# A gated MLP beside a long convolution: the filter's transposition moved from TensorE to DMAs, and the last down-projections split into column pairs

## The chip, the cores and the metric

The kernel runs on one core of one Trainium2 chip. The metric is device time in microseconds. The kernel before has a median of 190.6 us over 3 runs (190.31 to 190.84).

The engines that matter are TensorE (PE in the profile, its weight loads are PEld), VectorE (DVE), ScalarE (ACT), GpSimd (POOL) and SyncE (SP). Each executes its own instructions in the order in which they were written and waits on semaphores. DMAs are issued from SP, ACT or, in the changed kernel, also from POOL; a queue's issues stand in the order of the issuing engine's program.

## The reference

One input x of 2048 rows by 512 is normalised, and two branches use it:

```python
xn = layernorm(x)                                  # x = A_q, [1, 2048, 512]
# branch A: a 4-tap shift of k, times v, then a long causal convolution along the rows
kv = shift4(k, shift_k) * v
y  = irfft(rfft(pad(kv)) * rfft(pad(ssm_k)))[:2048] + kv * ssm_D
s  = xn * y
# branch B: a gated MLP, 512 -> 1792 -> 512
g  = silu((gelu(xn @ w_gate) * (xn @ w_up)) @ w_down)
out = x + s * g
```

The filter `ssm_k` is stored with its 512 channels as rows and the 2048 time steps as columns. The convolution works on tiles with time in partitions, so the filter has to be transposed before its first use.

## The kernel before, in words

**The gated MLP.** The 2048 rows are worked in four quarters q = 0 to 3 of 512. For each quarter and each of 14 column blocks m, `unit` (line 1190) runs four 128x512 matmuls with `Wg` and four with `Wu`, a GELU on ACT and a product on DVE that writes `HT`. The product reads the second matmul's result straight from PSUM (line 1203) or, for the units in the list UNITS, from a copy that ACT makes (line 1200). The first two units of q 0 are cut into 128-column matmuls. `down` (line 1206) then runs 14 matmuls with `Wd` for each of four row tiles. `Wd` comes in two loads, blocks 0 to 6 and 7 to 13. In the last quarter the last tile is done as 384 and 128 columns. In all there are 642 matmuls of 512 columns in gate, up and down, beside 14 of 384, 14 of 128, and the 64 of 128 of the first two units.

**The convolution.** It is done as a transform in two stages. Stage 1 (`stage1`, lines 950 and 959) multiplies data with time in partitions by the table `F1`, as two halves of 64 rows: 32 matmuls for the filter (H, from `HTr`) and 32 for kv (K, from `V`). ACT or DVE moves the results to SBUF; they go to DRAM scratch (`ZH` by ACT's queue, `ZK` by SP's) and come back regrouped as `BH` and `BK`. Stage 2 runs 16 passes of 16 small matmuls with the table `TF` (line 1028). Products of the spectra on DVE (lines 1131, 1154), eight inverse passes of 32 small matmuls, the scratch `ZI`, and 32 matmuls of 128x64 with `G1` (line 1270, called y here) end it. `kshift` (lines 1005 to 1013) makes kv on DVE: 28 operations of 128x2048, four groups of seven, the last of each group reading one load of v.

**The filter's transposition before.** Four loads bring `ssm_k` to `Hn` with channels in partitions. `h_transpose` (line 916) transposes it on TensorE, two bf16 values at a time as one fp32 value, 32 transposes of 128x128 into PSUM; five DVE and three ACT copies of 128x1024 bring it to `HTr`. A DVE operation on one partition (line 930, the fold) adds `ssm_D`.

**What sets the order.** Every piece of work is a task; the string SEQ lists all tasks in the order in which they are written into the engines' programs, and the table LAND holds the times at which a planner takes the loads to land. The string ORDER sets the order of the loads. The tracker `Trk` writes each engine's waits from the tiles that an instruction reads and writes. In the planner, loads are tasks of an engine of their own; in the program they are issued by SP, in one queue with its other DMAs.

The lines that carry matmuls through the helper `mm` all show as L642, and copies through `copy` as L633 (ACT) and L636 (DVE).

Of the kernel before, what the change touches and what calls it, by code (L numbers as in the profile page):

```python
# [25 lines left out]
ORDER = "x00 h0 x01 w0 D0 h1 w1 h2 h3 s0 k0 w2 x1 k1 k2 w3 d0 d1 v0 v1 k3 v2 v3 x2 x3"  # L26
SEQ = (
# [265 lines left out]
class Sched:  # L293
# [55 lines left out]
    def run(self):  # L349
# [4 lines left out]
        for name in SEQ.split():  # L354
# [17 lines left out]
            elif t.nbytes:  # L372
                en = t.end
                if eng == "ACT":
                    for l in order:
                        if l.eng == "loads" and l.end > t.start + 4300.0 and t.start < 48000.0:
                            l.end += self.TAKEN * min(1.0, (l.end - t.start - 4300.0) / 1000.0)
# [37 lines left out]
def build_kernel(nc, A_q, A_k, A_v, A_shift_k, A_ssm_k, A_ssm_D, B_w_gate, B_w_up, B_w_down, out):  # L415
    with ExitStack() as es0:
# [56 lines left out]
        top = place["at"]  # L473
        assert top <= 229344, top

        Hn = at("Hn", [128, KD, S_LEN], BF16, g_at)
        HTr = at("HTr", [128, NT // 2, 2 * DM], BF16, kk_at - 16384)
        skr_at = kac_at + 8192
        SKR = at("SKR", [128, DM * 4], BF16, skr_at)
# [131 lines left out]
        def psl(b):  # L611
            return b.slot
# [744 lines left out]
```

## Time and profile before

| what | value |
|---|---|
| median of 3 runs | 190.6 us |
| span of the profiled execution | 189.2 us |
| PE busy | 182.8 us, 97% |
| DVE busy | 165.5 us, 87% |
| ACT busy | 141.6 us, 75% |
| POOL busy | 10.4 us, 5% |
| moved by DMAs | 47.84 MB, mean 253 GB/s |

The span runs from the first to the last recorded instruction of the execution. The median of the runs is 1.4 us above it. "Busy" counts the time in which an engine has an instruction in work; overlapping instructions of one engine are counted once. The granted TensorE clock is 1.00 throughout but for the last slice. In the chain of work that ended last each piece is followed back to what released it. DMA rows give the microseconds from issue to landing.

### The profile page before, as it was taken

The page shows a single profiled execution, that of the slowest core. Times are in us where ns is not written, and L with a number is a line of the kernel's source. Part 1 is how long each engine was busy: PE and PEld are TensorE (multiplying, and loading weights), DVE is VectorE, ACT ScalarE, POOL GpSimd, SP SyncE. Part 2 cuts the span into 40 slices and gives each one's busy share as a digit, 9 for nine tenths or more (in the row PEclk, how much of TensorE's full clock was granted, in tenths as well). Part 3 has the DMA queues.
Part 4 walks back from the last instruction along what each step waited for, and adds up shares of the span by engine and source line. Part 5 has one row for each costly group of instructions (what it writes and reads, how often), then busy time and mean ns, then how long its engine had stood idle before and what let it go on. Part 6 is the DMA issues. An engine that isn't in the chain of part 4 may idle for free.

```text
span 189.2 us, 3591 instructions
## 1 busy us (share of the span) xinstructions
PE 182.8 (97%) x1406; PEld 80.6 (43%) x1418; DVE 165.5 (87%) x250; ACT 141.6 (75%) x196; POOL 10.4 (5%) x26
## 2 busy tenths in 40 slices
PE   7899999999999999999999999999999999999992
PEld 2685544544333334334444443433333344444441
DVE  6889999999999999978589599999999964658695
ACT  3749797998879798799638897998999575323971
POOL 5312302000000000022000000000000000000000
PEclk9999999999999999999999999999999999999998
DMA  5999999999584996557999997499345254908754
GB/s 177 319 381 297 366 380 360 402 415 297 166 309 150 335 287 229 166 187 235 301 310 173 333 322 251 144 299 326 135 162 170 97 181 146 376 36 283 268 186 153
DMA packets 36422, 47.84 MB, mean 253 GB/s; under 512 B 7347, under 2 KB 26039, under 8 KB 36406
## 3 DMA queue, kind: packets, MB, share of 16 engines
q1 hardware_dynamic: 29878, 39.23, 63.6%
q10 hardware_dynamic: 6528, 8.39, 12.8%
q8 instruction: 11, 0.18, 0.4%
q14 instruction: 5, 0.04, 0.1%
HBM read 27.39 MB, written 14.68 MB: 222 GB/s over the span
## 4 chain that ended last, share of the span: by engine, by line
PE 79%; DVE 15%; ACT 3%; issue 2%
PE psall L642 67%; PE psall L1028 6%; DVE KTM L1009 3%; DVE KAC L1011 2%; PE psall L916 2%; PE psall L950 2%; DVE HT L1203 1%; DVE G L1299 1%; PE psall L959 1%; PE psall L1270 1%; DVE G L1287 1%; DVE XN L965 1%; DVE G L1238 1%; DVE G L1237 1%; ACT XN L870 1%
## 5 line engine op out<-in xcount | busy, mean ns | idle before, releaser
L642 PE MATMUL psall<-xnT,Wu 128*128 128x512 bf16 (+1 forms) x248 | 56.0, 359 | 0.0
L642 PE MATMUL psall<-xnT,Wg 128*128 128x512 bf16 (+1 forms) x248 | 55.3, 359 | 0.5 <-DVE xnT L636 0.5
L642 PE MATMUL psall<-Wd,HT 128*128 128x512 bf16 (+2 forms) x226 | 50.3, 366 | 1.2 <-issue 0.8
L1194 ACT ACTIVATE GE<-psall 128x512 bf16<-128x512 f32 x54 | 31.7, 605 | 10.5 <-PE psall L642 10.0
L1203 DVE TENSOR_TENSOR HT<-psall,GE 128x512 bf16<-128x512 f32 x43 | 29.1, 685 | 8.0 <-PE psall L642 7.8
L642 PEld LDWEIGHTS psall<-xnT,Wu 128*128 128x128 bf16 x248 | 22.5, 98 | 26.0 <-issue 2.3
L642 PEld LDWEIGHTS psall<-xnT,Wg 128*128 128x128 bf16 x248 | 21.7, 98 | 26.7 <-issue 2.3
L642 PEld LDWEIGHTS psall<-Wd,HT 128*128 128x128 bf16 x238 | 21.4, 98 | 27.4 <-issue 5.4
L633 ACT ACTIVATE BO<-psall 128x1024 bf16<-128x1024 f32 x22 | 22.0, 1024 | 9.6 <-PE psall L1270 5.8
L1131 DVE TENSOR_TENSOR HSW<-KB,HSW 128x2048 bf16<-128x2048 bf16 x16 | 19.2, 1217 | 0.0
L633 ACT ACTIVATE HSW<-psall 128x1024 bf16<-128x1024 f32 x16 | 15.5, 1036 | 2.3 <-PE psall L1028 2.2
L633 ACT ACTIVATE KB<-psall 128x1024 bf16<-128x1024 f32 x14 | 13.8, 1028 | 2.6 <-PE psall L1028 2.4
L1011 DVE TENSOR_TENSOR KAC<-KAC,KTM 128x2048 bf16<-128x2048 bf16 x12 | 14.6, 1216 | 0.1
L1009 DVE TENSOR_TENSOR KTM<-KK,SKB 128x2048 bf16<-128x2048 bf16 x12 | 14.6, 1214 | 0.1
L633 ACT ACTIVATE AST<-psall 128x1024 bf16<-128x1024 f32 x12 | 12.3, 1023 | 1.9 <-PE psall L950 1.5
L1227 ACT ACTIVATE G<-psall 128x512 bf16<-128x512 f32 x12 | 7.2, 597 | 5.7 <-PE psall L642 4.5
L849 DVE BATCH_NORM_STATS2 stats<-X 128x6 f32<-128x512 bf16 x16 | 10.6, 672 | 0.5 <-DMA X<-in_A_q_dram 0.5
L1229 DVE SCALAR_TENSOR_TENSOR G<-G,psall 128x512 bf16<-128x512 bf16 x12 | 8.1, 680 | 3.0 <-ACT G L1227 3.0
L1131 DVE TENSOR_TENSOR KB<-KB,HSW 128x2048 bf16<-128x2048 bf16 x8 | 9.6, 1220 | 0.1
L1154 DVE TENSOR_TENSOR HSW<-HSW 128x2048 bf16<-128x2048 bf16 x8 | 9.5, 1217 | 0.0
L862 POOL TENSOR_TENSOR mv<-mv,NHALF 128x1 f32<-128x1 f32 (+1 forms) x7 | 5.3, 754 | 70.7 <-DVE mv L860 66.1
L633 ACT ACTIVATE X<-psall 128x1024 bf16<-128x1024 f32 x8 | 8.1, 1018 | 1.1 <-PE psall L959 1.0
(88 smaller groups left out, 163.4 us busy)
## 6 DMA issues: line engine op xcount, KB each, us to landing
BH<-ZH SPq DMA_DIRECT2D x8, 512.0 KB, 5.9
BK<-ZK SPq DMA_DIRECT2D x8, 512.0 KB, 5.8
HSW<-HSW SPq DMA_DIRECT2D x16, 256.0 KB, 3.1
ZI<-BO ACTq DMA_DIRECT2D x16, 256.0 KB, 2.9
BI<-ZI SPq DMA_DIRECT2D x8, 512.0 KB, 5.0
ZK<-AST SPq DMA_DIRECT2D x6, 512.0 KB, 3.4
Hn<-in_A_ssm_k_dram SPq DMA_DIRECT2D x4, 512.0 KB, 7.5
KK<-in_A_k_dram SPq DMA_DIRECT2D x4, 512.0 KB, 10.7
```

Of the source, the lines that this page charges most:

```text
L633: return h.activation(o, i, ACTF.Copy, scale=scale)
L642: return h.matmul(o, lhsT=l, rhs=r, start=st, stop=sp)
L849: t_stats[t] = op([("DVE", 670.0)], lambda e, h, t=t: h.bn_stats(stats[:, t, :], X[:, t, :]), r=[bX[q][t % 4]], w=[bst[t]], rr=[R_X[t]], w ...
L1009: op([("DVE", dur)], lambda e, h, j=j, m=m: h.tensor_tensor(KTM[:, m.slot, :, :], kk(j), sk(j), ALU.mult), r=need + [bSKB[j], a], w=[m], r ...
L1011: op([("DVE", dur)], lambda e, h, m=m: h.tensor_tensor(KAC[:, a.slot, :, :], KAC[:, a.slot, :, :], KTM[:, m.slot, :, :], ALU.add), r=[m], ...
L1028: trk.op("PE", lambda h: h.matmul(ps(s, i)[b, :], lhsT=wt(col)[a, :], rhs=data(col)[a, :], start=n < 16, stop=n >= len(todo) - 16, tile_po ...
L1131: return hd.tensor_tensor(pair(KB, *(2 * DM * z for z in slots())) if to else x, k, x, ALU.mult)
L1154: return hd.tensor_tensor(x, x, y, ALU.add)
L1194: op([("ACT", act(512))], lambda e, h: h.activation(GE[:, g.slot, :], bank(pg), ACTF.Gelu_apprx_tanh), r=[pg], w=[g], rr=lambda: R_bank(pg ...
L1203: op([("DVE", dve(512, 1))], lambda e, h: h.tensor_tensor(HT[:, q % 2, m, :], bank(pu), GE[:, g.slot, :], ALU.mult), r=[pu, g], w=[bHT[q][m]],
L1227: op([("ACT", act(n))], lambda e, h, g=g, pc=pc: h.activation(g, pc(), ACTF.Tanh, scale=0.5), r=[p], w=[bt], rr=lambda p=p: R_bank(p), ww= ...
L1229: op([("DVE", dve(512, 1))], lambda e, h, g=g, pc=pc: h.scalar_tensor_tensor(out=g, in0=g, scalar=1.0, in1=pc(), op0=ALU.add, op1=ALU.mult ...
```

## The change

1. **The filter's transposition.** The identity in fp32, the 32 transposes on TensorE and the eight copies to `HTr` go. Eight DMAs on SP's queue read `ssm_k` from DRAM, 128 channels by 1024 time steps (256 KB) each, and transpose it on the way into `HTT`, which lies in tiles 8 to 15 of `X` and `XN`. Two DMAs issued by POOL store `HTT` (1 MB each) to a new DRAM scratch `ZT`, and two more, which wait for both stores, load it back as `HTr` with the time steps regrouped (1 MB each). `HTr` now lies where `G` is later. The filter's stage 1 takes plain 512-column tiles, so its PSUM copies need no reordering.

2. **The last down-projections.** In the last quarter each 128x128 block of weights is split in two 128x64 blocks that go to the two column halves of the array, as y does. This holds for the 42 matmuls of 512 columns and the 14 of 384 columns; the 14 of 128 columns stay.

3. **The order.** ORDER, SEQ and LAND are new, and some dependencies between tasks are looser (the products of q 1 no longer wait for the filter's stage 1).

What the new order does on the engines:

- On TensorE the first K passes (8 matmuls, from v's first load) stand behind 128 and 140 of the 512-column gate and up matmuls, and the filter's stage 1 behind 152 to 200 of them; before, the filter's stage 1 stood behind 4 to 127 gate, up and down matmuls. The first down-projection (blocks 0 to 3) stands behind 196, its blocks 4 to 13 behind 200. The first stage-2 pass stands behind 287 (before 260), the last inverse pass behind 547 (before 534), the first y behind all 600 and eight paired matmuls (before behind 600).
- On DVE the fold stands behind 19 of the 28 kshift operations and 18 products of full units.
- On SP, the order of the loads is x, w0, x, D, w1, taps, halo, k0, h0, w2, h1, k1, h2, x1, h3, w3, h4, k2, h5, k3, h6, v0, h7. Behind h7 stand two stores `ZK<-AST`, which wait for ACT's copies of the first two K stage-1 results, and behind these the loads v1, v2, v3, wd0 and wd1. Before, all loads but the last two x stood ahead of the first `ZK` store.
- On POOL the four new DMAs stand behind the layernorm step of quarter 1 and ahead of those of quarters 2 and 3.

The core of the diff:

```diff
-ORDER = "x00 h0 x01 w0 D0 h1 w1 h2 h3 s0 k0 w2 x1 k1 k2 w3 d0 d1 v0 v1 k3 v2 v3 x2 x3"
+ORDER = "x00 w0 x01 D0 w1 s0 k0 h0 w2 h1 k1 h2 x1 h3 w3 h4 k2 h5 k3 h6 v0 h7 v1 v2 v3 d0 d1 x2 x3"
...
-        Hn = at("Hn", [128, KD, S_LEN], BF16, g_at)
-        HTr = at("HTr", [128, NT // 2, 2 * DM], BF16, kk_at - 16384)
+        HTr = at("HTr", [128, NT, DM], BF16, g_at)
+        HTT = [T[:, 8:16, :] for T in (X, XN)]
...
+        ZT = nc.dram_tensor("ZT", [S_LEN, DM], BF16, kind="Internal")
...
-        def load_h(k, ring):
-            load(f"h{k}", Hn[:, k, :], h_dr[:, k, :], [R_Hn[k]], [bHn[k]], 524288, ring)
+        def load_h(i):
+            h, k = i // KD, i % KD
+
+            def f(e):
+                o = HTT[h][:, :, 128 * k:128 * k + 128]
+                trk.dma("SP", lambda g: g.dma_start(out=o, in_=h_dr[:, k, 1024 * h:1024 * h + 1024], transpose=True), d_htt[i], w=[R_HTT[h][k]])
+            last_load[0] = S.add([("loads", T_ISSUE)], f, w=[bHTT[h][k]], nbytes=262144, land=float(LAND[f"h{i}"]))
...
-        def h_transpose(k):
...
-                        trk.op("PE", lambda h, o=o, src=src: h.transpose(o, src, ident32[:]), r=[R_Hn[k], R_id32], w=R_bank(pp[hf]), accum=True)
...
-                    return copy(e, h, HTr[:, 4 * hf:4 * hf + 4, 256 * k:256 * (k + 1)], bank16(pp[hf]).rearrange("p (t x) -> p t x", x=256))
...
+        for h in range(2):
+            def st(e, h=h):
+                dst = bass.AP(ZT, 1024 * h * DM, [[DM, 128], [128 * DM, 8], [1, DM]])
+                dma("POOL", dst, HTT[h], d_zt[h], R_HTT[h], [R_Z["T"][h]])
+            S.add([("POOL", P_ISSUE)], st, r=bHTT[h], w=[bZT[h]], nbytes=1048576)
+        d_htr = [dsem(f"d_htr{h}") for h in range(2)]
+        for h in range(2):
+            def ld(e, h=h):
+                src = bass.AP(ZT, 8 * h * DM, [[16 * DM, 128], [DM, 8], [1, DM]])
+                dma("POOL", HTr[:, 8 * h:8 * h + 8, :], src, d_htr[h], R_Z["T"], R_HTr[8 * h:8 * h + 8])
+            S.add([("POOL", P_ISSUE)], ld, r=bZT, w=[bHTr[h]], nbytes=1048576)
...
-            af = (down_tasks[q - 2] if q >= 2 else []) + (s1_tasks["H"] if q == 1 else [])
+            af = down_tasks[q - 2] if q >= 2 else []
...
+                        paired = q == NQ - 1 and c1 - c0 > 128
...
+                                if paired:
+                                    for i in range(2):
+                                        c = slice(64 * i, 64 * i + 64)
+                                        trk.op("PE", lambda h, m=m, i=i, c=c: h.matmul(pc()[c, :], lhsT=HT[:, q % 2, m, 128 * jt + 64 * i:128 * jt + 64 * i + 64], rhs=Wd[:, m, c0:c1], start=m == 0, stop=m == MF - 1, tile_position=(0, 64 * i)),
+                                               r=[R_HT[q % 2][m], R_Wd[m // 7]], w=R_bank(p), accum=True)
+                                    continue
```

More of the change, by code (lines that the diff above doesn't have):

```diff
@@ L373, in run @@
                 en = t.end
-                if eng == "ACT":
+                if eng in ("ACT", "POOL"):
                     for l in order:
                         if l.eng == "loads" and l.end > t.start + 4300.0 and t.start < 48000.0:
-                            l.end += self.TAKEN * min(1.0, (l.end - t.start - 4300.0) / 1000.0)
+                            l.end += self.TAKEN * t.nbytes / 500000.0 * min(1.0, (l.end - t.start - 4300.0) / 1000.0)
                 if eng == "SP":
@@ L559, in build_kernel @@
         R_KTM = [res(f"KTM{j}", KTM[:, j, :, :]) for j in range(1)]
-        R_Hn = [res(f"Hn{k}", Hn[:, k, :]) for k in range(KD)]
-        R_HTr = [[res(f"HTr{t}_{k}", HTr[:, t, 256 * k:256 * k + 256]) for k in range(KD)] for t in range(NT // 2)]
+        R_HTT = [[res(f"HTT{h}_{k}", T[:, :, 128 * k:128 * k + 128]) for k in range(KD)] for h, T in enumerate(HTT)]
+        for rh in R_HTT:
+            for r in rh:
+                for o in rh:
+                    if o is not r:
+                        r.ovl.remove(o)
+        R_HTr = [res(f"HTr{t}", HTr[:, t, :]) for t in range(NT)]
         R_SKR = res("SKR", SKR[:])
@@ L655, in build_kernel @@
         bWd = [B(f"Wd{i}") for i in range(2)]
-        bHn = [B(f"Hn{k}") for k in range(KD)]
-        bHTr = [[B(f"HTr{k}_{h}") for h in range(2)] for k in range(KD)]
+        bHTT = [[B(f"HTT{h}_{k}") for k in range(KD)] for h in range(2)]
+        bZT = [B(f"ZT{h}") for h in range(2)]
+        bHTr = [B(f"HTr{h}") for h in range(2)]
         bHD = B("HD")
@@ L926, in build_kernel @@
-        for k in range(KD):
-            h_transpose(k)
-        HT0 = HTr[0:1, 0, :].rearrange("p (d c) -> p c d", c=2)[:, 0, :]
+        d_zt = [dsem(f"d_zt{h}") for h in range(2)]
+        for h in range(2):
[4 more added lines that the diff above has]
+        d_htr = [dsem(f"d_htr{h}") for h in range(2)]
@@ L942, in stage1 @@
             a = B(f"A{x}{u}", pAST[x])
[L943 removed]
+            af = [] if x == "H" else kshift_tasks[:1] + [t_table]
             pp = [B(f"ps1{x}{u}_{i}", pC) for i in range(2)]
[L945 to L952 removed]
@@ L953, in stage1 @@
[L953 to L964 removed]
+            data, rdata = (HTr, R_HTr) if x == "H" else (V, R_V)
@@ new lines, in stage1, with halves @@
+            bdata = [bHTr[u // 4]] + ([bFold] if u == 0 else []) if x == "H" else [bKV[u // 2]]
+            bl = B(f"low{u}")
+            for i in range(2):
+                def halves(e, i=i):
+                    for b in range(2):
+                        k = slice(64 * b, 64 * b + 64)
+                        trk.op("PE", lambda h, b=b, k=k: h.matmul(ps(psl(pp[i]), b), lhsT=F1[k, :], rhs=data[k, 2 * u + i, :], start=True, stop=True, tile_position=(64 * b, 0)),
+                               r=[R_F1, rdata[2 * u + i]], w=[R_ps[psl(pp[i])][b]], accum=True)
+                s1_tasks[x].append(S.add([("PE", T_FWD)], halves, r=[bF1] + bdata, w=[pp[i]], lat=150.0, mode=2))
@@ L965, in stage1 @@
+            for i in range(2):
+                p = pp[i]
+                op(EV(1024), lambda e, h, p=p, i=i: copy(e, h, ast[x][a.slot][:, :, i, :], ps(psl(p)).rearrange("p (b d) -> p b d", b=2)), r=[p], w=[a] + ([bl] if x == "H" else []),
+                   rr=lambda p=p: R_ps[psl(p)], ww=lambda: [R_AST[x][a.slot]], after=af)
+            if x == "H":
                 op([("DVE", dve(1024, 2))], lambda e, h: h.tensor_tensor(ast[x][a.slot][:, 1, :, :], ast[x][a.slot][:, 1, :, :], ast[x][a.slot][:, 0, :, :], ALU.add), r=[bl], w=[a],
@@ L966, in stage1 @@
                    rr=lambda: [R_AST[x][a.slot]], ww=lambda: [R_AST[x][a.slot]])
-            for i in range(2 if x == "K" else 0):
-                p = pp[i]
-                op(EV(1024), lambda e, h, p=p, i=i: copy(e, h, ast[x][a.slot][:, :, i, :], ps(psl(p)).rearrange("p (b d) -> p b d", b=2)), r=[p], w=[a],
-                   rr=lambda p=p: R_ps[psl(p)], ww=lambda: [R_AST[x][a.slot]], after=af)
             def st(e):
```

68 lines of the change are left out of this document (17 added, 51 removed), and 44 rows, old and new, of the table SEQ.

## The prediction

> **What bounds the kernel now.** I read the page first, then the chain that ended last, the groups by line and window, and SP's own queue with its landings.
>
> ```profile
> span 189.2 us, 3591 instructions
> PE 182.8 (97%) x1406; PEld 80.6 (43%) x1418; DVE 165.5 (87%) x250; ACT 141.6 (75%) x196; POOL 10.4 (5%) x26
> ...
> by line: PE psall L642 66.8%; PE psall L1028 5.5%; DVE KTM L1009 3.0%; DVE KAC L1011 2.4%; PE psall L916 2.2%; PE psall L950 2.0%; issue 1.7%; DVE HT L1203 1.3%; DVE G L1299 1.1%; PE psall L959 1.1%; PE psall L1270 1.1%; DVE G L1287 1.0%; D
> ...
> 8.70 1.96 PE psall L642 x32
> 10.66 0.22 PE psall L892 x4
> ...
> 19.15 0.54 PE psall L959 x4
> ...
> 23.36 0.76 PE psall L959 x6
> 24.11 9.20 PE psall L642 x42
> ...
> 36.51 1.13 DVE KTM L1009
> 37.64 0.34 DVE HT L1200
> 37.98 1.14 DVE KAC L1011
> 39.11 0.60 DVE HT L1203
> ...
> 56.05 1.67 PE psall L642 x7
> ```
>
> TensorE is busy nearly throughout, and the chain is on it except from 35.8 to 56.05 us, where it runs through VectorE (kshift between the products of the units), and in the last ten microseconds. A 512-column matmul costs 9.20/42 = 0.219 us, a quarter matmul 1.96/32 = 0.061, a stage-1 group of four 0.54 and of six 0.76.
>
> ```profile
> 0.00:15.00 15.00, 13.27 (x111) 8.76 (x111) 11.98 (x36) 7.96 (x16) 4.89 (x19) 1.00 0.88 299
> 0.00:30.00 30.00, 28.27 (x196) 16.50 (x197) 26.53 (x58) 20.97 (x33) 7.32 (x23) 1.00 0.97 322
> 33.00:45.00 12.00, 11.81 (x70) 5.30 (x70) 12.00 (x18) 11.46 (x19) 0.00 (x0) 1.00 1.04 368
> 88.00:101.00 13.00, 12.68 (x101) 5.39 (x102) 9.88 (x17) 7.94 (x12) 1.01 (x1) 1.00 1.09 291
> 20.00:80.00 60.00, 59.71 (x306) 25.28 (x309) 59.83 (x81) 51.64 (x75) 1.36 (x2) 1.00 0.86 296
> 82.85:154.90 72.05, 71.42 (x781) 28.64 (x788) 63.51 (x83) 58.86 (x76) 2.02 (x2) 1.00 0.74 227
> 154.90:186.00 31.10, 30.58 (x169) 13.78 (x168) 22.29 (x35) 16.37 (x23) 0.00 (x0) 1.00 0.62 217
> ```
>
> After the length come the busy times of PE, weight loads, DVE, ACT and POOL, the granted clock, the DMA share and GB/s. Three resources are full at once early: DMAs to 45 us (9.7 MB by 30 us, then 368 GB/s), DVE from 20 to 80 us (59.8 of 60), PE always. So an edit that frees PE early gains only as far as DVE and the DMAs let the work move up.
>
> **The change, part by part.** The frame is the profiled execution: PE ends at 185.75 (its last row below), the span at 189.2, the median 1.4 above the span. I re-time PE's order by stretches and keep those 3.45 us of tail.
>
> *Transposes off TensorE.*
>
> ```profile
> L916 PE MATMUL psall<-ident,Hn 128*128 128x128 f32 x24 | 3.7, 285 | 0.0
> ...
> L636 DVE COPY HTr<-psall 128x1024 bf16<-128x1024 bf16 x5 | 3.3, 682 | 0.2 <-PE psall L916 0.2
> ...
> L849 DVE BATCH_NORM_STATS2 stats<-X 128x6 f32<-128x512 bf16 x4 | 2.5, 674 | 0.0
> ...
> L986 POOL COPY SKB<-SKR 128x512 bf16<-128x512 bf16 x4 | 2.4, 654 | 7.6 <-DMA SKR<-in_A_shift_k_dram 7.6
> ```
>
> The chain gives this line 2.2% of the span, 4.2 us over 32 transposes; the first two rows here are of 8.7 to 56.05 us, the statistics of 15 to 52. That is the most that PE can gain. But the first eight run while nothing else is ready, before quarter 0 is normalised, so I leave PE's first gate matmul at 8.70. From there to the filter's first pass PE has 64 quarter matmuls (3.9), 152 matmuls (33.3), 24 transposes of xn (0.055 each, 1.3) and two K groups (1.1): 48.3 us. DVE loses the five copies, and reaches the fold after 19 kshift operations (1.14 each, 21.7), 18 products (eleven of 0.60, seven of 0.34, 9.0) and some 4.5 us of layernorm (four statistics are 2.5 of it). It starts when taps and the first k are there: 3.5 MB of loads are 11.7 us at the 299 GB/s of the first 15, 2.0 to land (below), 2.4 for POOL's copies of the taps, 16 us. So the fold is at 51: DVE is level with PE, so this is the earliest, not a cushion.
>
> *The filter's new path.*
>
> ```profile
> 31.20 1.86 SPq L615 DMA_DIRECT2D V<-in_A_v_dram  x2
> 33.11 3.05 SPq L1039 DMA_TRANSPOSE MI<-TFA  x1
> ...
> 48.42 1.21 SPq L1039 DMA_TRANSPOSE MI<-TFB  x1
> 57.61 0.41 SPq L615 DMA_DIRECT2D ZK<-AST  x1
> ...
> 88.57 4.88 SPq L884 DMA_TRANSPOSE xnT<-XN  x1
> ...
> ZH<-XN ACTq DMA_DIRECT2D x4, 512.0 KB, 3.4
> ...
> Wd<-in_B_w_down_dram SPq DMA_DIRECT2D x2, 896.0 KB, 13.7
> ...
> 169.88 1.94 ACT L633 ACTIVATE BO<-psall 128x1024 bf16<-128x1024 f32 x2 [1.71 <-PE psall L1270]
> ```
>
> A transposing DMA takes SP 1.21 us for 128 KB and 4.88 for 512 KB, so 2.44 for each of the eight, 19.5 in all against 0.41 for a plain one. SP can have issued h7 near 30 us; the data come later. Up to h7 the loads are 10.35 MB, plus the first 1.05 MB store. With 9.66 MB by 30 us and 368 GB/s after, that is moved by 34.7. The window from 88 to 101 us, with two transposes of xn among plain DMAs, moved 291 GB/s at full DMA share: 13 x (1 - 291/368) = 2.7 us lost for 1.05 MB, so 5.4 for the filter. I take half (other gaps may be in that window): 37.4, and 2.0 to land (3.4 of a 512 KB store less 1.4 of moving): 39.4. Then the second store and the first load, one after the other: 1.05 MB at 368 GB/s is 2.85, with 2.0 fixed 4.9 each, and 0.4 to issue each: HTr's first half lands at 50 (47 to 53). I take PE's first filter pass at 50, 1.7 after it could.
>
> The Trainium skill (Advanced Engine Details and Errata, X-Bar Transpose) says that transposing DMAs on this chip are as fast as regular ones. By that the 2.7 fall away, HTr lands at 47.3 and PE loses nothing here; the window's 291 GB/s speaks for some loss.
>
> *Loads behind a wait.* This is the edit that decides. On SP two ZK stores now stand before v1 to v3 and wd0, wd1, and they wait for the first K results. By DVE, kv of the first group is ready 8.7 us before the fold (six kshift operations, 6.8; four products, 1.9), at 42.3; two K groups with 12 matmuls between end at 46.2; ACT's last two copies take 1.9: the stores go out at 48.5, the loads by 52, where the loads before were all issued by 33. They carry 4.45 MB (ZK 1.05, v 1.57, Wd 1.83). Beside them run HTr's second half (1.05) and ZH stores: 7.1 MB with three of these, 19.2 us at 368 GB/s; wd1 lands near 69, 63 if it has all of the bandwidth, 72 with five ZH stores. The stores will not give way: ZH lands in 3.4 us beside loads that take 13.7. PE wants wd1 after 48 more matmuls (10.5) and the 32 filter matmuls (4.2), at 50 + 14.7 = 64.7. The bounds are 0 and 7; I take 4.0, near the upper sum. DVE's later uses of v1 to v3 (from 65 us) are covered.
>
> *To the end.* From there to the first stage-2 pass 87 matmuls (19.1) and six K groups (3.2): 22.3. The middle, first stage-2 pass to last inverse, took 72.05 us with 274 matmuls; it now has 260: minus 3.1, 69.0. DVE then fills 63.5 of 69 less some regrouping and ACT 58.9; the cover is thin, so 0 to 2 for the range.
>
> ```profile
> 169.19 1.00 PEld L1270 LDWEIGHTS psall<-BI,G 128*64 128x64 bf16 x12 [0.42 <-DVE HT L1203]
> ...
> 182.09 3.66 PE L642 MATMUL psall<-Wd,HT 128*128 128x512 bf16 x29
> ...
> 169.26 1.42 PE psall L1270 x12
> ...
> 174.67 0.60 PE psall L1270 x4
> ```
>
> *Column pairs.* Twelve y matmuls took 1.42 and four 0.60, so a further pair costs (1.42 - 0.60)/4 = 0.205 us, no more than one full matmul, with two weight loads of 1.00/12 = 0.083 each inside. The 56 pairs cost nothing; for the 384-column ones the loads (0.167) and columns (0.164) are level. The entry to a y group, 0.60 - 0.41 = 0.19, falls away four times: -0.7. The tail is 30.85 (154.9 to 185.75), less 13 matmuls (2.85) and 0.7: 27.3.
>
> The Trainium skill (TensorEngine Tiling (Array Packing), Restrictions) says that column tiling disables Fast Weight Load, which speaks against pairs; the y rows above, which pay for it already, show no loss in pace.
>
> *Sum.* 50 + 14.7 + 4.0 + 22.3 + 69.0 + 27.3 = 187.3 against 185.75: +1.55. On the median: 192.2 us.
>
> **The rivals.**
>
> *The loads arrive in time.* If wd1 takes the bandwidth first (63 us), nothing waits at the first down-projection and the sum is 183.3, or 181.6 with HTr before 48.3: 2.4 to 4.1 faster, 186.5 to 188.2. For it: once h7 has landed the queue of loads is empty, so the filter's store and load have the DMAs to themselves. Against it: the ZH stores start just as the loads do. It decides at 64.7 us for wd1.
>
> *The regrouping is late.* The four DMAs are POOL's first here, in a stretch where DVE is never idle. No row prices their issue; a POOL copy of 0.65 us is one end. If each of the three in the chain (second store, two loads) waits for one or two DVE operations of 1.14, the first half lands 2.3 to 5 us later, at 52 to 55, and the fold holds up DVE, which has nothing to spare. By 55, the Wd wait shrinks to nothing, since PE then asks at 69.7, and the sum is 188.3, to 190 if the second half is late too: 193 to 195.5.
> The Trainium skill (SBUF — State Buffer, SBUF: two separate sides) has this as a rule: POOL's DMA descriptors are held up while DVE runs two-port operations. No run here shows it yet.
>
> *The pairs do not overlap.* Then 42 x 0.219 + 14 x 0.164 = 11.5 us more, 203.7. The y rows speak against it.
>
> **How the numbers follow.** Late Wd loads 0.48, loads in time 0.33, late regrouping 0.14, serial pairs 0.03, the rest for faults in the middle. About 0.3% (0.6 us) is what a measurement can tell from no change. Of the first, 0.05 ends within that and 0.03 below; of the second 0.03 ends within. Faster 0.30 + 0.03 = 0.33, within 0.3% 0.05 + 0.03 = 0.08, slower 0.40 + 0.19 = 0.59. The likeliest gives 192.2, its own range 190 to 195. The range over the first three is 187 to 196.5: below it lie only loads and HTr both at their earliest, above it serial pairs.
>
> **What would show it.** The line of the fp32 transposes is gone and DVE's copies to HTr too. In SP's queue the first ZK store stands near 48 us and wd1's issue after it, with a wait on ACT. PE idles before its first Wd matmuls (64 to 70 us), released by a DMA of Wd; in the first rival that idle time is nil, in the second PE and the fold wait for HTr. The first filter pass is at 50, the first stage-2 pass at 91, the last inverse near 160. The paired rows run at 0.21 to 0.22 us a pair. I am wrong if the first Wd matmul waits for nothing, if transposing DMAs take far more than 2.44 us of SP or throttle the other loads so that Wg and Wu are late from 15 to 30 us, or if the middle does not keep the pace of 72 us for 274 matmuls.

## The result

The changed kernel is slower: 203.5 us median (199.7 to 205.7, 4 runs) against 190.7 us for the kernel before on the same chip, and a ratio of 1.052 with an interval of 1.047 to 1.057. The ratio is taken from the two lower of the four runs, 9.9 us above the kernel before; the two upper ones, of which one is the profiled execution (205.7 us), are left out of it, so the trace below accounts for some 5 us more than the ratio stands for. The forecast was 192.2 us, with a range of 187 to 196.5. The direction was right, though not for the reason given; the size was far too small.

First the page of the profile after. The rows PE and PEclk have one digit for each fortieth of the span, the busy share and the granted clock in tenths.

```profile
span 203.9 us, 3660 instructions
PE 184.5 (90%) x1442; PEld 77.6 (38%) x1442; DVE 165.5 (81%) x250; ACT 136.3 (67%) x188; POOL 13.3 (7%) x29
PE   7799979997089839999999999999999999999993
PEclk9999999999769976999999999999999999999999
```

PE was busy 97% of the span before and is at 90%. It does about as much as before, but it has holes at 50 to 57 us and at 70 to 75 us, and behind each the granted clock is low for some microseconds.

The waits of PE in the profile after (microseconds in total, times, the longest):

```profile
PE psall L950 <- DMA HTr<-ZT: 7.0, 1, 7.0
PE psall L950 <- DVE XN L642: 4.0, 1, 4.0
PE psall L648 <- DMA Wg<-in_B_w_gate_dram: 1.9, 2, 1.5
```

None of them is for `Wd`, the wait on which the forecast was built. The chain of work that ended last (start, length, what) shows how the two long ones come about:

```profile
30.60 9.32 DMA XN<-in_A_ssm_k_dram
...
39.95 3.94 issue
...
43.91 5.25 DMA ZT<-XN
...
49.44 7.26 DMA HTr<-ZT
...
56.84 1.04 PE psall L950 x4
...
62.95 10.56 DMA ZH<-XN
...
73.60 1.23 DVE XN L642
...
74.89 1.04 PE psall L950 x4
```

*The first hole* is the filter's new path: transposed tiles, store to DRAM, load from it, all one after the other. The loaded half lands at 56.7 us and PE, free since 49.9, starts the filter's stage 1. The chain shows the seventh transposing DMA, issued at 30.60 us. The store waits for the eighth as well, issued at 34.05, and the view of its tile has that one landing 9.6 us later, at 43.6:

```profile
L819 SPq DMA_TRANSPOSE XN<-in_A_ssm_k_dram x1: 3636/3636/3636, 34.1 to 34.1; - x1
...
DMA to landing us min/median/max: 9.6/9.6/9.6
```

So most of the 3.94 us of "issue" is the wait for this landing; POOL's store goes out 0.3 us behind it.

*The second hole* begins as a slow store. The results of the filter's stage 1 go through four staging tiles in SBUF, which are free again only when the `ZH` stores that read them have landed. The store that the chain shows takes 10.56 us. The copy on DVE that wants its tile waits, and PE waits for that copy, since it empties the PSUM pair that PE needs.

SP's queue at that time says what the store has beside it (start, length of the issue, line, what):

```profile
49.14 0.90 SPq L621 DMA_DIRECT2D ZK<-AST  x2
50.09 1.95 SPq L621 DMA_DIRECT2D V<-in_A_v_dram  x3
52.08 7.21 SPq L621 DMA_DIRECT2D Wd<-in_B_w_down_dram  x2
```

A small transposing DMA (`MI<-TFA`, from 59.34 us) follows them. No run moves it alone, but the DMAs move 379 and 389 GB/s in the two slices of the page from 61 to 71 us, no less than plain loads elsewhere (362 in a window below). That speaks for the bytes beside the store and against a slow transfer.

*The clock* is read from windows (start to end, length, busy time and instructions of PE, weight loads, DVE, ACT and POOL, granted clock, DMA share, GB/s):

```profile
57.00:61.00 4.00, 4.00 (x15) 0.88 (x12) 0.64 (x2) 2.66 (x3) 0.00 (x0) 0.62 1.00 389
75.00:79.00 4.00, 4.00 (x12) 1.03 (x10) 3.97 (x5) 1.94 (x2) 0.00 (x0) 0.50 0.15 47
79.00:85.00 6.00, 6.00 (x29) 2.00 (x28) 4.44 (x6) 4.31 (x5) 0.00 (x0) 0.87 0.79 267
...
103.43:172.59 69.16, 69.16 (x774) 27.40 (x774) 59.34 (x69) 58.81 (x77) 1.01 (x1) 1.00 0.75 237
172.59:200.68 28.09, 27.70 (x211) 14.03 (x211) 22.00 (x36) 14.83 (x19) 0.00 (x0) 1.00 0.73 239
```

PE is busy in the whole of the first three windows, but at 0.62, 0.50 and 0.87 of its pace. The pace lost is 4.00 x 0.38 + 4.00 x 0.50 + 6.00 x 0.13 = 4.3 us. The last two windows are the middle and the tail of the prediction's sum: from the first stage-2 pass at 103.43 us on, next to nothing is lost.

So the profiled execution is 14.7 us longer than the one before (203.9 against 189.2): its first stage-2 pass comes 20.6 us later (103.43 against 82.85), and the rest is 5.9 us shorter, as the moved matmuls and the pairs were to make it.

### The profile page after: what moved, and what is told of

It is laid out like the page before. It is cut to its first block, busy times and chain, and to the rows that moved or that the text cites. A ratio compares the mean times of both kernels' runs of the same rounds, so it can differ in the third digit from the quotient of the medians.

```text
span 203.9 us, 3660 instructions
## 1 busy us (share of the span) xinstructions
PE 184.5 (90%) x1442; PEld 77.6 (38%) x1442; DVE 165.5 (81%) x250; ACT 136.3 (67%) x188; POOL 13.3 (7%) x29
## 4 chain that ended last, share of the span: by engine, by line
PE 58%; DMA 17%; SPq 11%; DVE 6%; issue 3%; ACT 2%; POOL 1%; ACTq 0%; POOLq 0%; DVEq 0%
PE psall L648 47%; SPq L819 9%; DMA ZH<-XN 5%; PE psall L1017 5%; DMA XN<-in_A_ssm_k_dram 5%; PE psall L950 4%; DMA HTr<-ZT 4%; DMA ZT<-XN 3%; SPq L621 2%; PE psall L1213 2%; DMA X<-in_A_q_dram 2%; ACT BO L639 1%; DVE G L1296 1%; DVE G L1284 1%; DVE G L1235 1%
## 5 line engine op out<-in xcount | busy, mean ns | idle before, releaser
L648 PE MATMUL psall<-xnT,Wu 128*128 128x512 bf16 (+1 forms) x248 | 57.9, 367 | 0.7 <-ACT xnT L639 0.7
L648 PE MATMUL psall<-Wd,HT 128*128 128x512 bf16 (+1 forms) x182 | 41.5, 373 | 0.0
L639 ACT ACTIVATE BO<-psall 128x1024 bf16<-128x1024 f32 x21 | 20.7, 1025 | 9.7 <-PE psall L1267 6.7
L648 PEld LDWEIGHTS psall<-Wd,HT 128*128 128x128 bf16 x182 | 16.3, 99 | 22.8 <-issue 5.7
L950 PE MATMUL psall<-HTr,F 64*128 64x512 bf16 x32 | 6.4, 493 | 11.2 <-DMA HTr<-ZT 7.0
L639 ACT ACTIVATE KB<-psall 128x1024 bf16<-128x1024 f32 x15 | 14.9, 1021 | 2.2 <-PE psall L1017 1.9
L639 ACT ACTIVATE HSW<-psall 128x1024 bf16<-128x1024 f32 x15 | 14.6, 1030 | 1.7 <-PE psall L1017 1.7
L998 DVE TENSOR_TENSOR KTM<-KK,SKB 128x2048 bf16<-128x2048 bf16 x12 | 14.6, 1217 | 0.0
L1000 DVE TENSOR_TENSOR KAC<-KAC,KTM 128x2048 bf16<-128x2048 bf16 x12 | 14.6, 1217 | 0.0
L639 ACT ACTIVATE XN<-psall 128x1024 bf16<-128x1024 f32 x5 | 5.0, 1022 | 13.1 <-PE psall L950 11.4
L639 ACT ACTIVATE AST<-psall 128x1024 bf16<-128x1024 f32 x12 | 12.2, 1024 | 2.3 <-PE psall L950 2.0
L1213 PE MATMUL psall<-Wd,HT 128*64 128x512 bf16 (+1 forms) x112 | 12.7, 366 | 0.0
L642 DVE CAST XN<-psall 128x1024 bf16<-128x1024 f32 x3 | 3.7, 1224 | 8.0 <-DMA ZH<-XN 4.6
```

Source lines behind the costliest of these rows:

```text
L639: return h.activation(o, i, ACTF.Copy, scale=scale)
L648: return h.matmul(o, lhsT=l, rhs=r, start=st, stop=sp)
L950: trk.op("PE", lambda h, b=b, k=k: h.matmul(ps(psl(pp[i]), b), lhsT=F1[k, :], rhs=data[k, 2 * u + i, :], start=True, stop=True, tile_posit ...
L998: op([("DVE", dur)], lambda e, h, j=j, m=m: h.tensor_tensor(KTM[:, m.slot, :, :], kk(j), sk(j), ALU.mult), r=need + [bSKB[j], a], w=[m], r ...
L1000: op([("DVE", dur)], lambda e, h, m=m: h.tensor_tensor(KAC[:, a.slot, :, :], KAC[:, a.slot, :, :], KTM[:, m.slot, :, :], ALU.add), r=[m], ...
L1213: trk.op("PE", lambda h, m=m, i=i, c=c: h.matmul(pc()[c, :], lhsT=HT[:, q % 2, m, 128 * jt + 64 * i:128 * jt + 64 * i + 64], rhs=Wd[:, m, ...
```

## The experiments

Three theories stood at the start. A: the filter is late, and POOL's part of its way is slow (it reads the chain's 3.94 us as POOL's). B: the `ZH` stores are slow because v1 to v3 and Wd, which now stand behind the `ZK` stores, move at the same time. C: the holes are followed by a low clock, which costs more on top. The rival to all of them: the new order is worse in itself.

### The filter's way: who issues it, and what of it is dear

**The four scratch DMAs issued by SP.**

```diff
-                dma("POOL", dst, HTT[h], d_zt[h], R_HTT[h], [R_Z["T"][h]])
+                dma("SP", dst, HTT[h], d_zt[h], R_HTT[h], [R_Z["T"][h]])
...
-                dma("POOL", HTr[:, 8 * h:8 * h + 8, :], src, d_htr[h], R_Z["T"], R_HTr[8 * h:8 * h + 8])
+                dma("SP", HTr[:, 8 * h:8 * h + 8, :], src, d_htr[h], R_Z["T"], R_HTr[8 * h:8 * h + 8])
```

> The four DMAs that store and load the regrouped filter are issued by SP instead of POOL; nothing else changes. Theory A (POOL is late: 3.94 us pass there between the landing of the last transposed tile and the second store's issue, and the load lands 7.3 us after its issue): SP issues the store within 0.5 us of the landing, the first half of HTr lands at 51 to 53 us instead of 56.7, and the stall of 7 us ahead of the filter's first pass falls to 1 to 3 us; time 4 to 6 us less than the changed kernel, 196 to 199. Rival (the wait is DMA bandwidth, whoever issues): HTr still lands past 55 us and the time stays within 2 us of the changed kernel. The second stall, ahead of the task that needs the slot of a ZH store, is not touched by either.

Measured: 199.2 us, ratio to the kernel before 1.045 (1.041 to 1.049). Its chain:

```profile
42.96 4.43 DMA ZT<-XN
...
47.41 5.17 DMA HTr<-ZT
...
52.71 0.61 PE psall L950 x4
...
58.65 8.94 DMA ZH<-XN
```

HTr lands at 52.58, in the window that A gave, 4.1 us earlier than from POOL, and the stall is 2.8 us. Store and load are 0.8 and 2.1 us shorter. Of the rest, 0.7 us is the landing of the last transposed tile (42.94 instead of 43.6), and 0.5 us are the two gaps between a landing and the next issue (0.02 us each from SP, 0.3 from POOL). So the delay of 3.94 us that A puts down to POOL is not there. The landing is late by itself: the DMAs moved nothing from 42 to 44 us (the windows stand below), and of the sixteen signals in the trace that make up this landing fifteen came by 42.07 us and one at 43.61. Why is not shown. Nor are the load's 2.1 us POOL's: with plain loads (next), where no `ZK` store and no v runs beside it, the load from POOL takes 5.3 us.

The time came out 0.2 us above the window, but it is not 4 to 6 us below the changed kernel: the ratios, 1.045 and 1.052, have intervals that overlap, and differ by 1.4 us. The second hole is still there (a store of 8.94 us), as expected.

**Plain loads instead of transposing ones, scratch kept.**

```diff
...
-                o = HTT[h][:, :, 128 * k:128 * k + 128]
-                trk.dma("SP", lambda g: g.dma_start(out=o, in_=h_dr[:, k, 1024 * h:1024 * h + 1024], transpose=True), d_htt[i], w=[R_HTT[h][k]])
+                o = HTT[h].rearrange("p t d -> p (t d)")[:, 1024 * k:1024 * k + 1024]
+                trk.dma("SP", lambda g: g.dma_start(out=o, in_=h_dr[:, k, 1024 * h:1024 * h + 1024]), d_htt[i], w=[R_HTT[h][k]])
```

> The changed kernel with the eight loads of the filter as plain DMAs into the same staging tiles, so without transposing; the store to the DRAM scratch and the load from it stay, issued by POOL (filter untransposed, only the time means something). It parts the two halves of the filter's new path. If the transposing is what is dear (8 issues of 1.5 to 4.3 us on SP, DMAs full at low rates): the staging tiles land by 32 to 36 us instead of 41.7, HTr by 48 to 51, 192 to 196. If the store and load are (each 4.4 us at best, one after the other, and 4.2 MB more to move): HTr still past 54, 199 to 202.

Measured: 194.2 us, ratio 1.015 (1.009 to 1.020). Its DMAs on POOL:

```profile
37.72 0.91 POOL L621 DMA_DIRECT2D ZT<-XN  x1 [6.96 <-DMA XN<-in_A_ssm_k_dram]
43.07 1.12 POOL L621 DMA_DIRECT2D HTr<-ZT  x2 [4.45 <-DMA ZT<-XN]
```

A window of it, with the granted clock, DMA share and GB/s last, and behind it three of the changed kernel:

```profile
14.00:26.00 12.00, 10.73 (x53) 4.84 (x52) 9.61 (x11) 3.48 (x6) 2.30 (x4) 1.00 1.07 362
```

```profile
14.00:26.00 12.00, 11.52 (x57) 5.19 (x56) 9.60 (x11) 4.08 (x8) 1.57 (x3) 1.00 1.10 261
38.00:42.00 4.00, 4.00 (x21) 1.80 (x19) 4.00 (x7) 1.70 (x4) 0.00 (x0) 1.00 0.97 191
42.00:44.00 2.00, 2.00 (x12) 0.68 (x11) 2.00 (x2) 1.28 (x3) 0.09 (x1) 1.00 0.00 0
```

With plain loads the last tile lands at 37.4 us instead of 43.6, the second store goes out at 37.72 instead of 43.91, the load at 43.07 instead of 49.44, and PE does not wait for HTr at all, with POOL issuing and the scratch in use. So it is the transposing that makes the filter late: 6.2 us at the store, in a stretch where DMAs that are full by their share move 261 GB/s instead of 362. The Trainium skill (Advanced Engine Details and Errata, X-Bar Transpose) has transposing DMAs as fast as regular ones; here they are not, and the measurement decides.

**The loads ahead of the ZK stores, POOL still issuing.** In SEQ the tasks 44 to 48 (v1, v2, v3, wd0, wd1) move up behind task 54.

```diff
-503 218 213 524 54 154 480 504 505 484
+503 218 213 524 54 44 45 46 47 48 154 480 504 505 484
```

> Only the order of SP's queue changes: v1 to v3 and both halves of Wd are issued ahead of the two ZK stores, so they no longer wait for the first K results. Theory B (the second stall, 4 us, is there because the ZH stores move beside these 3.4 MB of loads and beside HTr's second half): the loads are issued by 40 us and landed by 55, the first ZH store lands within 3 to 5 us instead of 10.6, the second stall is below 1 us; 4 to 6 us less than the changed kernel, if the regrouping is not pushed back by the same loads; if it is, HTr lands 2 to 5 us later than 56.7 and the gain is eaten up. My forecast (Wd late) expects 0 from this edit by itself, since Wd did not hold PE up.

Measured: 204.2 us, ratio 1.071 (1.067 to 1.076). The issues of v1 to wd1 end at 41.5 us. Its chain:

```profile
44.16 8.84 DMA ZT<-XN
...
53.28 10.58 DMA HTr<-ZT
...
64.00 1.04 PE psall L950 x4
```

B held: the `ZH` stores land in 2.8 to 3.6 us, and there is no second hole. But the loads now run beside the filter's store and load, which take 8.84 and 10.58 us instead of 5.25 and 7.26, so PE waits 14 us for HTr. I had expected 2 to 5 us of that; it was 7.

**Both edits.**

> Both edits: regrouping issued by SP, and the loads ahead of the ZK stores. If A and B both hold and are independent: HTr at 52 to 54 us, no second stall, 9 to 12 us less than the changed kernel, 191 to 194. If the loads only push the regrouping back, no better than the first edit alone, 196 to 199.

Measured: 197.0 us, ratio 1.034 (1.028 to 1.039); the best form of the changed kernel that still transposes by DMA, but 3 us above the window for two independent edits. It lies in the window of the other case, but not by that case's mechanism: HTr is not pushed back. On SP the loads stand behind the store's and the load's waits, so v1 to wd1 go out from 47.2 to 53.1 us, hardly earlier than in the changed kernel. HTr lands at 51.2, and the second `ZH` store still takes 8.8 us:

```profile
56.20 8.77 DMA ZH<-XN
```

### The second hole, with the filter out of the way

**The filter loaded in place**, without transposing and scratch, all other work in the changed kernel's order.

```diff
-                o = HTT[h][:, :, 128 * k:128 * k + 128]
-                trk.dma("SP", lambda g: g.dma_start(out=o, in_=h_dr[:, k, 1024 * h:1024 * h + 1024], transpose=True), d_htt[i], w=[R_HTT[h][k]])
+                o = HTr[:, 2 * i:2 * i + 2, :].rearrange("p t d -> p (t d)")
+                trk.dma("SP", lambda g: g.dma_start(out=o, in_=h_dr[:, k, 1024 * h:1024 * h + 1024]), d_htt[i], w=R_HTr[2 * i:2 * i + 2])
```

> The filter is loaded by plain DMAs straight into HTr, without transposing and without the DRAM scratch (so the filter is left untransposed, and only the time means something); the order of all other work is that of the changed kernel. Theory A with C (late filter, and a lowered TensorE clock behind the stall that it makes): no stall ahead of the first filter pass, granted clock 1.00 through 50 to 65 us, first filter pass at 48 to 50; if the later ZH stall stays, 193 to 196, if it goes with the traffic of the regrouping, 187 to 190, which is at or below the kernel before. Rival (the new order is worse in itself, wherever the filter comes from): over 198.

Measured: 194.5 us, ratio 1.020 (1.016 to 1.023). The first filter pass is at 47.9 and waits for nothing, so A and B are separate: the second hole stays.

```profile
52.74 9.64 DMA ZH<-XN
...
63.76 1.04 PE psall L950 x4
```

**The same, with v1 to v3 and Wd ahead of the ZK stores** (the two diffs together).

> The changed kernel with the filter loaded in place (no transposing, no scratch; filter untransposed) and with v1 to v3 and Wd issued ahead of the ZK stores: what the new order gives when neither the filter nor the ZH stores are late. Theory B (the second stall comes from ZH stores sharing the DMAs with v, Wd and ZK): the stall of 1.4 and 2.0 us and the low clock of 63 to 67 us seen with the filter in place alone go, first stage-2 pass at 86 to 88 instead of 92.2, 188 to 190, level with the kernel before. Rival (the new order has other losses): 193 to 195 as with the filter in place alone.

Measured: 188.7 us, ratio 0.990 (0.987 to 0.993), the one kernel with the new order that is faster than the kernel before. Wd goes out on SP at 25 us, and the granted clock is 1.00 throughout. The row of Wd in SP's queue, and the first stage-2 pass on PE:

```profile
25.33 6.86 SPq L621 DMA_DIRECT2D Wd<-in_B_w_down_dram  x2
```

```profile
86.67 0.43 PE L1017 MATMUL psall<-BH,TF 32*32 32x512 bf16 x16
```

The four `ZH` stores up to 60 us land in 2.8 to 3.8 us. This settles B and the rival: nothing is wrong with the new order as such, if neither the filter nor these stores are late. The kernel itself is of no use beyond that, since it leaves the filter untransposed.

**Both edits, with plain loads, scratch kept** (the diffs of the first three kernels above together).

> The same on the kernel with both edits (regrouping issued by SP, loads ahead of the ZK stores; 197.0): plain loads in place of the transposing ones, scratch store and load kept. With the filter in place and the loads first the time was 188.7, so 8.3 us are shared between transposing and scratch. If transposing holds most of them: 189 to 191.5; if the scratch traffic does: 194.5 to 197.

Measured: 195.8 us, ratio 1.024 (1.019 to 1.029). Here the scratch holds most of the difference, where with POOL issuing and the old place of the loads it held none. The reason is the queue: on SP v1 to v3 and Wd stand behind the waits of the scratch's store and load, so that Wd goes out at 43.9 to 48.2 us instead of 25.3 to 32.2, and the store collides again:

```profile
53.86 9.41 DMA ZH<-XN
```

In the three kernels where the filter is in time but the loads are not (194.2, 194.5 and 195.8 us) the store takes 9.4 to 9.6 us and the first stage-2 pass stands at 92.2 to 92.8; where the loads are early as well, it stands at 86.67. So the second hole with the clock behind it is worth 5.5 to 6.1 us.

**v2 and v3 put off behind the ZK stores**, on the kernel with both edits. In SEQ the tasks 45 and 46 move far down.

```diff
-524 54 44 45 46 47 48 154 480
+524 54 44 47 48 154 480
...
+45 46
```

> The kernel with both edits (197.0), but of the loads ahead of the ZK stores v2 and v3 (1.05 MB, first used at 75 us) are put behind the first small transposing DMA of the running product, so that they are issued some 8 us later, after the ZK stores. Theory B, in the form in which it is left (a ZH store takes 9 us whenever v, Wd, ZK and HTr's second half are still on the DMAs when it goes out at 56 us, however they came to be late): 1.05 MB less on the DMAs ahead of it is some 2.8 us at 370 GB/s, so the first ZH store lands in 6 us instead of 8.8, the stall of 1.8 us goes, and with it the low clock of 66 to 70 us; 193 to 195. Rival (the store is slow for another reason than these loads): landing stays at 8 to 9 us, 196 to 198.

Measured: 201.3 us, ratio 1.057 (1.055 to 1.059): a miss, above both windows. The two loads go out at 60.9 us, while the first two `ZH` stores (57.3 and 58.6 us) are still on their way. These take 8.0 and 10.5 us, and the next two 12.0 and 10.7. Copies on ACT and DVE wait for them: the chain has the third, which ACT waits for, and PE waits 3.6 us for DVE's copy behind the second:

```profile
62.66 11.97 DMA ZH<-X
```

That a store is slow beside these loads holds; that a part of them can be put off at a gain does not. Against the kernel with both edits the first stage-2 pass is 4.9 us later in the traces (98.80 against 93.86). The filter's first pass is 1.3 us later (52.66 against 51.34; its last tile lands 1.1 us later, again by one signal of sixteen). Its hole is 3.0 instead of 1.8 us and has a low clock behind it (0.50 from 54 to 57 us), which with the other hole's makes 1.9 us more of lost pace (3.4 against 1.5 us, by windows of 1 us). The waits around the second hole are 1.8 us longer (4.5 against 2.8).

### The clock

**PE kept at work through the first hole.**

```diff
+FILL = {(1, 0): 28}
...
+                    if x == "H" and (u, i) in FILL:
+                        for _ in range(FILL[u, i]):
+                            trk.op("PE", lambda h: mm(h, ps(psl(pp[i]), 0), F1[:], V[:, 0, :], True, True), r=[R_F1, R_V[0]], w=R_ps[psl(pp[i])], accum=True)
```

> The changed kernel with 28 filler matmuls (128 x 512, their result is overwritten) put on PE just ahead of the filter's first pass, so that PE works through its wait of 7 us. Theory C (the granted clock goes down because PE has stood idle for more than about 2 us, and comes back only after some us of work): the clock stays at 1.00 from 50 to 62 us, the four Wu matmuls behind the first filter pass take about 1.0 us instead of 1.89, and the second stall, still there, keeps its own low clock; 1 to 2 us less than the changed kernel. Rival (the low clock belongs to the traffic or to these matmuls, not to the idle time): 0.5 to 0.7 stays in 52 to 60 us and the time does not fall.

Measured: 201.8 us (201.1 to 202.8), ratio 1.057 (1.054 to 1.061). PE's rows at the hole (the lines are numbered one higher than in the changed kernel up to the added lines, and four higher behind them):

```profile
49.66 6.21 PE L649 MATMUL psall<-V,F 128*128 128x512 bf16 x28
57.24 0.61 PE L954 MATMUL psall<-HTr,F 64*128 64x512 bf16 x4 [1.38 <-DMA HTr<-ZT]
57.78 1.04 PE L649 MATMUL psall<-xnT,Wu 128*128 128x512 bf16 x4
```

The four Wu matmuls behind the first pass take 1.04 us instead of 1.89, and the clock is 1.00 until the second hole, which was not filled and has its low slice. So C holds for the clock: it goes down because PE stood idle. In time the gain is not shown: the median is 1.8 us below the changed kernel's, but that kernel's own runs are 6 us apart, and by the ratios the two can't be told apart.

The other runs show how little idle time is enough. In the kernel with SP issuing, one hole of 2.8 us is followed by about 3.4 us at half clock (by windows of 1 us: 0.68, 0.50, 0.50 and 0.62 from 53 to 57 us). In the kernel with both edits the hole of 1.8 us at 51 us is followed by none, while 0.7 and 1.8 us close together, at 64 and 66 us, are. The Trainium skill (TensorE: Matmul & The Clock Gate, What's actually happening) gives the two states, half and full, and a window of about 3.4 us that is watched; the half and the 3.4 us agree with these windows. The same section of the Trainium skill has the lower state set in after at least one idle window of about 3.4 us; here 2.8 us were enough, and the measurement decides. No single limit for the length of a hole fits these runs.

### The parts alone, in the order of the kernel before

**The column pairs alone.**

```diff
+                                if q == NQ - 1 and c1 - c0 > 128:
+                                    for i in range(2):
+                                        c = slice(64 * i, 64 * i + 64)
+                                        trk.op("PE", lambda h, m=m, i=i, c=c: h.matmul(pc()[c, :], lhsT=HT[:, q % 2, m, 128 * jt + 64 * i:128 * jt + 64 * i + 64], rhs=Wd[:, m, c0:c1], start=m == 0, stop=m == MF - 1, tile_position=(0, 64 * i)),
+                                               r=[R_HT[q % 2][m], R_Wd[m // 7]], w=R_bank(p), accum=True)
+                                    continue
```

> The kernel before with one part of the change alone: the last down-projections are column pairs of 128 x 64. The forecast's term: the pairs cost nothing and four entries to y groups fall away, 0.7 us faster (ratio 0.996). Bounds: 0 if the entries do not show, 11.5 us slower if pairs do not overlap.

Measured over 12 runs: 190.4 us against 191.0, ratio 0.9973 (0.996 to 0.9986), that is 0.5 us faster (0.3 to 0.8). This version beats both kernels.

**The transposes made cheap.**

```diff
-                    for j in range(4):
-                        o = bank(pp[hf])[:, 128 * j:128 * (j + 1)]
-                        src = Hn[:, k, :].bitcast(FP32).rearrange("p (a t) -> p t a", t=NT // 2)[:, 4 * hf + j, :]
-                        trk.op("PE", lambda h, o=o, src=src: h.transpose(o, src, ident32[:]), r=[R_Hn[k], R_id32], w=R_bank(pp[hf]), accum=True)
+                    trk.op("PE", lambda h: mm(h, bank(pp[hf]), ident32[:].bitcast(BF16)[:, 1::2], Hn[:, k, 512 * hf:512 * hf + 512], True, True), r=[R_Hn[k], R_id32], w=R_bank(pp[hf]), accum=True)
```

> The kernel before, with each group of four fp32 transposes of the filter replaced by one bf16 matmul of 128 x 512 (eight groups; the filter's values are wrong by this, only the time means something). Loads, PSUM tiles and copies stay as they were; only PE's early work falls, by about 4.2 us less eight times 0.22, so 2.5 us. If the head is bound by PE, 2 to 2.5 us faster than before, 188.5 to 189. If those transposes ran in time that PE had to spare (as leaving them out altogether, 192.5, suggests), the time is 190 to 192.

Measured: 190.5 us against 190.9, ratio 0.998 (0.9962 to 0.9998): 0.4 us for 2.5 us of PE work taken away. A new wait of 1.2 us for DVE's product (L1200) stands on PE's queue in its stead.

**The transposes and copies left out.** The loads go straight to HTr, and neither the transposes nor the copies behind them are issued.

```diff
-            load(f"h{k}", Hn[:, k, :], h_dr[:, k, :], [R_Hn[k]], [bHn[k]], 524288, ring)
+            load(f"h{k}", HTr[:, :, 256 * k:256 * k + 256], h_dr[:, k, :].rearrange("p (t x) -> p t x", x=256), [x[k] for x in R_HTr], [bHn[k]], 524288, ring)
```

> The kernel before, in its old order, with the filter's transposing left out altogether: the filter goes by the same number of plain DMAs straight into HTr, the 32 transposes on TensorE and the copies behind them are not issued (the filter stays untransposed, only the time means something). This is the most that taking the transposes off TensorE can bring without a new order. If PE bounds the head of the kernel, 4.2 us faster (the line's share of the chain). Rival (the head is held by DVE's kshift chain and the loads, and the first transposes run where nothing else is ready): 0 to 2 us faster.

Measured: 192.5 us, ratio 1.006 (1.004 to 1.009): slower than with the transposes, outside what either theory gave. The longest of PE's waits (its line 955 is the filter's stage 1):

```profile
PE psall L642 <- DVE xnT L636: 1.7, 2, 1.4
PE psall L955 <- ACT XN L633: 1.6, 1, 1.6
```

PE comes earlier to work whose inputs are not there yet. But the loads differ too (pieces of 512 bytes in SBUF: 30135 packets under 2 KB against 26039), so this run alone does not price the transposes; the one above does.

## Why the prediction was wrong, point by point

- **What bounds the kernel.** "An edit that frees PE early gains only as far as DVE and the DMAs let the work move up" was right, and stronger than I made it: in the old order 2.5 us of early PE work are worth 0.4 us. The 4.2 us of the chain were an upper bound, as said.
- **The filter's new path**: failed, in the term for the transposing (2.7 us) and in "HTr's first half lands at 50". PE was ready at 49.9, 1.6 us behind the 48.3 of the forecast (it had waited 1.9 us for `Wg`), but the half landed at 56.7, 3.7 us past my upper bound. The last tile landed at 43.6 instead of 39.4. With plain loads it lands at 37.4, where the forecast without its 2.7 gives 36.7, so the transposing cost 6.2 us: I had halved the 5.4 that the window in the trace of before gave, and the whole of it was nearer. From 14 to 26 us alone, 261 GB/s instead of 362 are 12 x (1 - 261/362) = 3.3 us. The eight issues on SP took 1.49 to 4.26 us each, 23.6 in all, instead of 19.5. From the landing to the end of the load it was 13.1 us instead of 10.6: the store took 5.25 us, and the load, priced at 4.9 us with the DMAs to itself, took 7.26, because it reached the DMAs together with the `ZK` stores and v1 to v3.
- **Loads behind a wait**: the edit was the right one to look at, but the step failed at the sentence "The stores will not give way". The v loads went out when forecast (by 52 us), those of Wd from 52.1 to 59.3, and the two halves of Wd landed 14.6 and 21.0 us after their issues, at 66.7 and 73.9. That is late for the 64.7 at which PE was to ask, as forecast; but both holes came ahead, PE asked only at 77.5, and that wait was nil. The load traffic was paid elsewhere: by the `ZH` stores, whose slow landing blocks staging tiles, DVE's copy and PE. I took 3.4 us from the median of a group. The trace of the kernel before had the answer in the view of that tile: its first two `ZH` stores, at 28 and 31 us beside the loads, landed after 7.1 and 7.9 us, and the median of the group hid them.

```profile
L615 ACTq DMA_DIRECT2D ZH<-XN x1: 380/380/380, 27.9 to 27.9; - x1
L615 ACTq DMA_DIRECT2D ZH<-X x1: 371/371/371, 30.9 to 30.9; - x1
...
DMA to landing us min/median/max: 7.1/7.5/7.9
```

- **Not in the sum at all**: the low clock behind each hole, 4.3 us. The clock was 1.00 throughout before, so no row of that trace could price it; that a kernel with holes would lose it was not considered.
- **From the filter's first pass to the first stage-2 pass** I had 14.7 + 22.3 = 37.0 us without a wait; with the filter and the loads early it is 86.67 - 48.56 = 38.1. In the changed kernel it is 46.6: 38.1, and 4.0 and 0.3 of waits, and 4.3 of clock.
- **The middle** (69.0) was right: 69.2. **The pairs** were right: 0.5 us (0.3 to 0.8) instead of 0.7. The tail was 28.1 instead of 27.3, of which 0.4 is a wait for `BI`.
- **The sum.** PE ends at 200.68 instead of 187.3: 6.8 for the late filter, 5.6 behind it (9.6 us more than 37.0, less the 4.0 for Wd that fell away), 0.2 in the middle and 0.8 in the tail: 13.4. What put the forecast above the kernel before was the 4.0 for Wd (without it the sum is 183.3 against 185.75). It did not occur, so that the direction came out is luck.
- **The rivals.** "The regrouping is late" was nearest in time, with 0.14: it put the first half 2.3 to 5 us late, and it was 6.7 us late. The reason was another. 4.2 us were there before POOL had anything to issue, POOL issued 0.3 us after each landing, and the load's excess came from its company on the DMAs. What is left for POOL against SP is 0.5 us at the issues and 0.8 at the store. The rule that it cites (the Trainium skill, SBUF — State Buffer, SBUF: two separate sides) might explain a part of that; DVE was at work all the time between 38 and 44 us, but no run changed DVE's work, so it is not shown. "The loads arrive in time" (186.5 to 188.2) is close to what the new order gives once filter and loads are early: 188.7. "The pairs do not overlap" fell.
- **The range** took each fault by itself. Two holes in one chain, each with its clock, added up past it.

What stays open: why the changed kernel's own runs are 6 us apart, and why one signal of the last tile's landing is 1.5 us behind the others.

## What to carry to other kernels

When a load is moved behind a wait, ask not only who needs it, but which stores will be on the DMAs when it goes out, and what their buffers hold up; take a store's landing from the rows that had such company, not from the median of its group. Work taken off TensorE early in a kernel is worth only as much as its inputs are early, so measure it first by making that work cheap. In these runs a hole of 2.8 us or more in TensorE's queue cost its length and then 1.5 to 2.8 us for the low clock behind it, and so did two shorter ones close together; a lone one of 1.8 us cost its length only.

## What the runs showed of the hardware that I had not expected

- A 512 KB store from ACT's queue lands in 2.8 to 3.8 us when SP's loads are through, and in 6.2 to 10.6 us (12.0 with v2 and v3 put off) beside v1 to v3, Wd and the `ZK` stores (4.5 MB in all) from SP's. The Trainium skill (DMA: Bandwidth & Descriptors, Queues, rings and completion order) has each DMA engine take turns between the queues that have work for it; the slow stores do not contradict that, but no run here tells it from other ways of sharing.
- Eight transposing DMAs of 256 KB, among plain loads, take 1.5 to 4.3 us of SP each (plain ones 0.42 to 0.67, but for two of 3.3 and 3.9) and bring the DMAs from 362 to 261 GB/s while their share stays full.
- The same 1 MB store and load took 5.25 and 7.26 us from POOL and 4.43 and 5.17 us from SP. With plain loads ahead, and no `ZK` store and no v beside them, they took 5.1 and 5.3 us from POOL, so the load's difference is not POOL's.
